# Multi-head attention on one core: the reciprocals' broadcast as four copies, the last set's lines on VectorE, and another order of the closing products

## The chip, the cores and the metric

The kernel runs on one core of one Trainium2 chip. The metric is the device time of one execution in microseconds. A core has TensorE (PE) for matrix products, VectorE (DVE), ScalarE (ACT) and GpSimd (POOL) for elementwise work, and SyncE (SP), which issues DMA copies. ScalarE and GpSimd can issue DMA copies too. All engines run at once and wait for one another by semaphores. Each executes its own instructions in the order in which the program has them.

## The reference

```python
B, S, D, H = 1, 2048, 448, 16          # bf16 inputs x, wqkv, wo
Dh = D // H                            # 28
qkv = (x @ wqkv).reshape(B, S, 3, H, Dh).transpose(2, 0, 3, 1, 4)
q, k, v = qkv[0], qkv[1], qkv[2]
scores = jnp.einsum("bhqd,bhkd->bhqk", q, k) * (Dh ** -0.5)
p = softmax(scores, axis=-1)
o = jnp.einsum("bhqk,bhkd->bhqd", p, v)
return o.transpose(0, 2, 1, 3).reshape(B, S, D) @ wo
```

## The kernel before

The sixteen heads form four groups of four (HG), each head in a band of 32 of the 128 partitions (HP). The 2048 queries form four chunks of 512 (QW). One group with one chunk of queries is a set; there are 16 sets (NSET), and the keys come in 16 tiles of 128. For each set, head and key tile TensorE makes a block of 128 x 512 scores (`emit_s`, L726), something turns it into weights of the softmax, and TensorE multiplies the weights by the values into one PSUM bank, the tile o (`do_pv`, L1069). One row of each head's band of o collects the sum of the weights, the softmax's denominator.

The weights are made in two ways. ScalarE takes two score blocks at once from the PSUM pairs a0 and a1 and writes exponentials into a tile pt (`do_exp`, L924); it does so 358 times, which is 716 of the 1024 blocks. VectorE makes the other 308 blocks from the banks d0, d1 and m: it writes the score as an integer that is the bit pattern of an approximate power (tile I, `do_a`, L939), and the weight is the sum of three such terms, each the first one with a number added to the integer. Four blocks of one set form a chain. The second and third term of a chain are the tiles called J. The third, and in some chains the second, is one addition on VectorE over four blocks (`do_add`, L1010). In the chains that are marked far, the second term is made elsewhere: GpSimd fills J with the number (`far_chain`, L975) and issues an accumulating DMA that adds I to it (`accumulate`, L986). A chain is far if at least FAR = 30 blocks of its set are left when it begins, and not in set 0.

When a set's products are complete, `finish_set` (L1084) queues its closing steps: VectorE copies o out of PSUM (`evac`, L1096); SyncE gathers the four denominator rows into a 128 x 16 tile (`gather`, L1101); VectorE takes reciprocals (`recip`, L1105); SyncE writes them to DRAM (`scatter`, L1110) and reads them back, each head's row repeated over its 32 partitions (`spread`, L1115, tile rr); GpSimd multiplies (`mul`, L1118) and writes the normalized output, tiles xs or OTL. Four of those, one for each group, are the input of the output projection of a query chunk (`oproj_job`, `quarters` at L301, bank m, VectorE's copy at L593, SyncE's store at L596).

The order of all instructions is written by a planner inside the kernel while the program is built. It keeps a clock for each engine, an estimated duration for each step and a time at which its result lands, and emits whatever can go next (`best`, `pick_pe`, `pick_dve` and so on, L1128 to L1244). `add` takes the step's cost, `land` the time until a DMA's result is there, `lag` a wait that is put before the step. A number changed in one step therefore moves the steps of all engines from there on. In `finish_set` the plan has these numbers: gather 0.6 and a landing of 3.0 (1.5 in the last two sets that are closed there), a lag of 2.5 before the reciprocal (0.3), scatter 0.35 and 1.1, spread 0.5 and a landing of 8.0 (6.0), multiply 1.3.

The last set (number 15) is not closed by `finish_set`. Near the end the planner queues early products of the output projection for the last query chunk, those of groups 0 to 2 (`early_jobs`, L1251), for four blocks of 128 queries in the banks d0, d1, m and one half of a pair. They start when fewer than 12 blocks are left for the first three, and when none is left for the fourth. The steps at L1285 to L1328 close the set: VectorE copies o in two halves, TensorE transposes the denominators (L1307), VectorE takes reciprocals (L1309), TensorE spreads them over the bands (L1313), VectorE multiplies (L1316, tile OTf), then whatever is left of the early products is emitted by `filler`, then TensorE adds group 3's product to each bank (L1323), VectorE and ScalarE copy the four banks out (L1325, L1327), and SyncE stores them in two pairs (L1328).

Of the kernel before, what the change touches and what calls it, by code (L numbers as in the profile page):

```python
# [39 lines left out]
def kernel(  # L40
# [7 lines left out]
    nc = tc.nc  # L48
# [4 lines left out]
    HP = 32  # L53
    G = 4
    HG = 4
    CC = 4
    CK = D // CC
    QW = 512
# [9 lines left out]
    XB = 4  # L68
# [9 lines left out]
    NJ = 4  # L78
    FAR = 30
    FIRST = 1  # L80
    AGE = 2.5
    SPLITQ = {1: ([0], [1, 2, 3]), 2: ([0, 1, 2, 3],), 3: ([0, 1, 2, 3],)}
    ACC_LAND = 5.6
    DRAIN = 10
    WARM = 0.52
    CL = NQC - 1
    NSET = G * NQC
# [7 lines left out]
    out_perm = out2.rearrange("(p t) d -> p t d", t=NKT)  # L95
# [140 lines left out]
    held = {}  # L236
# [3 lines left out]
    def add(eng, dur, emit, **k):  # L240
        op = Op(eng, dur, emit, **k)
        ops[eng].append(op)
        return op

    def ready(op):
        if cnt["step"] < op.gate or (op.acq == "m" and op.gives[0][0] == "O" and left() < 12):
            return None
        if op.acq == "m" and op.pri > 5 and ("KN0", NQC - 1) not in evt:
            return None
        r = 0.0  # L250
        for n in op.need:
# [513 lines left out]
    def left():  # L765
        return sum(len(q) for s in remain for q in remain[s])
# [39 lines left out]
    def d_more(s, t, acting):  # L806
        got, taken = [], []
        for b in d_banks(t):
            if not dve_ok(t, len(got)):
                break  # L810
            p = d_pick(s, t, acting, taken)
            if p is None:
                break
            step = take(*p)
            taken_by[step[0]][step[1]] += 1
            ch = chain["cur"]
            if ch is None:
                ch = chain["cur"] = {"I": wk.tile([P, HG * QW], I16, name="I4", bufs=NCH), "s": step[0], "n": 0,
                                     "got": [0] * NTERM, "m": None, "next": 0, "done": 0, "acc": 0.0, "far": False}
                chain["all"].append(ch)  # L820
                ch[1] = wk.tile([P, HG * QW], I16, name="J1", bufs=NJ)
                if sum(len(q) for q in remain[step[0]]) >= FAR and step[0] >= FIRST:
                    ch["far"] = True
                    far_chain(ch)
            taken.append(ch["next"])
            ch["next"] = 1 - ch["next"]
            ch["n"] += 1
            pd = bank_tile(b)
            got.append((b, pd, step, ch, ch["n"] - 1, max(t, res[b])))
# [254 lines left out]
    def finish_set(s, end):  # L1084
        g, c = set_gc(s)
        evt[("Oset", s)] = (end, "PE")
        cur["oset"] = s + 1
        cur["o_open"] = False
        o = cur["o"]
        if s == NSET - 1:  # L1090
            return
        st = {}

        def evac():
            st["o_sb"] = wk.tile([P, QW], F32, name="o_sb", bufs=2)
            nc.vector.tensor_copy(out=st["o_sb"][:], in_=o[:])  # L1096

        def gather():
            st["den"] = wk.tile([P, HG * QW // P], F32, name="den")
            n = P // HG  # L1100
            nc.sync.dma_start(out=st["den"][:], in_=st["o_sb"][Dh:P:HP, :].rearrange("i (p f) -> i p f", p=n))  # L1101

        def recip():
            st["rec"] = wk.tile([P, HG * QW // P], F32, name="rec")
            cur["shared"] = nc.vector.reciprocal(out=st["rec"][:], in_=st["den"][:])  # L1105

        def scatter():
            n = P // HG
            st["scr"] = dram.tile([HG, QW], F32, name="scr")
            nc.sync.dma_start(out=st["scr"][:].rearrange("h (p f) -> (h p) f", p=n), in_=st["rec"][:])  # L1110

        def spread():
            scr = st["scr"]
            st["rr"] = wk.tile([P, QW], F32, name="rr", bufs=1)
            nc.sync.dma_start(out=st["rr"][:], in_=scr[:].unsqueeze(1).to_broadcast([HG, HP, QW]))  # L1115

        def mul():
            m = nc.gpsimd.tensor_tensor(out=otile(g, c), in0=st["o_sb"][:], in1=st["rr"][:], op=ALU.mult)  # L1118
            after_shared(m)

        add("DVE", 0.61, evac, need=[("Oset", s)] + ([("OT",) + set_gc(s - 2)] if s > 1 else []), gives=[("osb", s)], rel="o", pri=-5)
        add("SP", 0.6, gather, need=[("osb", s)], gives=[("den", s)], land=3.0 if s < NSET - 2 else 1.5, pri=2)
        add("DVE", 0.16, recip, need=[("den", s)], gives=[("rec", s)], pri=50, lag=2.5 if s < NSET - 2 else 0.3, port=True)
        add("SP", 0.35, scatter, need=[("rec", s)], gives=[("scr", s)], land=1.1, pri=2)
        add("SP", 0.5, spread, need=[("scr", s)], gives=[("rr", s)], land=8.0 if s < NSET - 2 else 6.0, pri=2)
        add("POOL", 1.3, mul, need=[("rr", s)], gives=[("OT", g, c)], pri=60, port=True)

    def best(eng, t):  # L1128
# [119 lines left out]
    def late(op):  # L1248
        return op.gives and op.gives[0][0] == "O" and op.gives[0][1] == CL - 1

    def early_jobs(todo):  # L1251
        held.setdefault("early", [None] * XB)
        c = ORDER[-1][1]

        def mm(tq, bank, gg):
            if gg == 0:
                t = pair_tile(bank)[:, QW:2 * QW] if bank[0] == "a" else bank_tile(bank)[:]
                held["early"][tq] = t
            quarters(held["early"][tq][:, 0:D], otile(gg, c)[:, tq * P:(tq + 1) * P], WO[:, gg, :], gg == 0, False)

        for tq, bank in todo:
            for gg in range(G - 1):
                add("PE", 0.192, lambda tq=tq, bank=bank, gg=gg: mm(tq, bank, gg),
                    pri=2000 + tq, cols=D, need=[("OT", gg, c)] + ([("E", tq, gg - 1)] if gg else []), gives=[("E", tq, gg)],
                    acq=bank if gg == 0 else None)

    while cur["oset"] < NSET or ("E", 0) not in held or any(not late(op) and op.gives[0][0] != 'E' for e in ops for op in ops[e]) or any(k[0] == "O" for k in held):
        if left() < 12 and chain["cur"] is None and "early" not in held:
            early_jobs(enumerate(("d0", "d1", "m")))
        if left() == 0 and ("E", 0) not in held:  # L1270
            held[("E", 0)] = True
            early_jobs([(XB - 1, s_bank())])
        e = min(free, key=lambda n: free[n])
        t = free[e]
        end, nxt = pick[e](t)
        if end is not None:
            free[e] = end
            stuck = 0
            continue
        others = min(free[n] for n in free if n != e)  # L1280
        free[e] = max(t + 0.02, nmin(nxt, others))
        stuck += 1
        assert stuck < 40000, (t, cur, left(), pending, [(o.eng, o.need, o.acq) for q in ops.values() for o in q])
# [3 lines left out]
    o = cur["o"]  # L1287
    HW = QW // 2
    banks = held["early"]
    more = [op for op in ops["PE"] if op.gives[0][0] == "E"]  # L1290

    def filler(n):
        for op in more[:n]:
            op.emit()
        del more[:n]

    osb_last = [VT[1][0, hf].rearrange("p t e -> p (t e)").bitcast(F32) for hf in range(2)]
    rT = [wk.tile([P, 2, HG], F32, name=f"rT{hf}", bufs=1) for hf in range(2)]
# [11 lines left out]
    for hf in range(2):  # L1310
# [3 lines left out]
                                 lhsT=rT[hf][:, k, i:i + 1].to_broadcast([P, HP]), rhs=identf[:],  # L1314
                                 start=True, stop=True, tile_position=(0, HP * i))
        nc.vector.tensor_tensor(out=OTf[hf][:], in0=osb_last[hf], in1=work_ps[hf][:, HW:2 * HW], op=ALU.mult)  # L1316
    filler(12)
    rest = sorted({op.gives[0][2] for op in ops["PE"] if late(op)})
    for hf in range(2):
        osb = wk.tile([P, 2 * QW], BF16, name="pt", bufs=NPT)[:, 0:2 * D].rearrange("p (t d) -> p t d", t=2)  # L1320
        for k in range(2):
            tq = 2 * hf + k
            quarters(banks[tq][:, 0:D], OTf[hf][:, k * P:(k + 1) * P], WO[:, G - 1, :], False, True)  # L1323
            if k == 1:
                nc.vector.tensor_copy(out=osb[:, k, :], in_=banks[tq][:, 0:D])  # L1325
            else:
                nc.scalar.copy(out=osb[:, k, :], in_=banks[tq][:, 0:D])  # L1327
        nc.sync.dma_start(out=out_perm[:, c * XB + 2 * hf:c * XB + 2 * hf + 2, :], in_=osb)  # L1328
    for tq in rest:
        ps = pair_tile("a0" if tq % 2 else "a1")[:, 0:QW]  # L1330
        for gg in range(G):
# [38 lines left out]
```

## Time and profile before

| | us |
|---|---|
| three runs | 366.99, 363.5, 365.86 |
| median | 365.86 |
| the profiled execution | 365.38 |
| its span, first to last instruction | 363.5 |
| TensorE busy | 339.5 (93%) |
| VectorE busy | 333.4 (92%) |
| ScalarE busy | 340.8 (94%) |
| GpSimd busy | 174.8 (48%) |
| software DMA queue (GpSimd's) | 42.8% of 16 engines |
| SyncE's DMA queue | 9.9% of 16 engines |

The span leaves out 1.88 us of the profiled execution that lie around the first and the last instruction. Matmuls are pipelined, so TensorE's busy time says little by itself. In the views, a line has the start, the time it covers, the engine, the source line, the operation with its output and inputs, how many instructions are merged, and in brackets the idle time of the engine before it and what ended that. Idle time of an engine that is not the bottleneck costs nothing. Some of the steps that the change touches, as the profile has them:

| step | count | mean |
|---|---|---|
| L975 GpSimd fills J | 57 | 1064 ns |
| L986 GpSimd issues the accumulate of 512 KB | 57 | 915 ns; 4.9 us to landing (median) |
| L1010 VectorE adds, J from I | 97 | 758 ns |
| L1115 SyncE issues the broadcast of 256 KB | 15 | 554 ns (median) |
| L1118 GpSimd multiplies | 15 | 1415 ns for the 12 of tiles xs |

### The profile page before, as it was taken

What the parts mean: (1) busy time and instruction counts of PE and PEld (TensorE: products, weight loads), DVE (VectorE), ACT (ScalarE), POOL (GpSimd) and SP (SyncE); (2) the same over time, 40 slices, a digit from 0 to 9 for tenths busy, and PEclk for the clock granted to TensorE, in tenths of its full rate; (3) what the DMA queues carried; (4) which work ended last, traced back from release to release, by engine and by line L of the source; (5) the groups of instructions that cost most, each with busy time, mean ns of one, the idle gap of its engine ahead of it and who ended that gap; (6) DMA issues with size and microseconds to landing.
All of it is one profiled execution on the core that took longest, in us unless ns stands there. A gap on an engine that the chain in (4) does not pass through costs nothing.

```text
span 363.5 us, 11157 instructions
## 1 busy us (share of the span) xinstructions
PE 339.5 (93%) x4500; PEld 110.4 (30%) x4500; DVE 333.4 (92%) x615; ACT 340.8 (94%) x373; POOL 174.8 (48%) x217
## 2 busy tenths in 40 slices
PE   8999999999999999999889999988789899999975
PEld 4433233322234233232222222222222222222223
DVE  7789999999999999999999899999899999999933
ACT  4689999999999999999999999999899999999961
POOL 8951453644534374545655465447445244544310
PEclk9999999999999999999999999999999999999988
DMA  8510064664636356463668463486847467585741
GB/s 248 134 44 14 22 125 91 117 120 93 131 66 141 83 104 137 101 134 92 135 133 170 93 118 83 95 168 140 160 108 153 90 129 144 123 166 130 158 98 52
DMA packets 23260, 42.20 MB, mean 116 GB/s; under 512 B 7720, under 2 KB 13992, under 8 KB 23208
## 3 DMA queue, kind: packets, MB, share of 16 engines
q0 software_dynamic: 8720, 30.29, 42.8%
q1 hardware_dynamic: 13448, 10.18, 9.9%
q10 hardware_dynamic: 1040, 1.02, 0.9%
q8 instruction: 35, 0.57, 0.7%
q14 instruction: 17, 0.14, 0.1%
HBM read 7.58 MB, written 1.96 MB: 26 GB/s over the span
## 4 chain that ended last, share of the span: by engine, by line
ACT 39%; PE 30%; DVE 15%; issue 8%; DMA 6%; POOL 0%; DVEq 0%; ACTq 0%
ACT pt L924 38%; PE a L726 11%; PE o L1069 8%; DVE I L939 6%; DMA J<-I 5%; PE m L301 5%; DVE J L1010 3%; PE m L294 3%; DMA xs<-in_x_dram 1%; DVE KA L334 1%; DVE V L575 1%; DVE V L562 1%; DVE QA L456 1%; PE a L294 1%; PE d L301 1%
## 5 line engine op out<-in xcount | busy, mean ns | idle before, releaser
L924 ACT ACTIVATE pt<-a 128x1024 bf16<-128x1024 f32 x358 | 329.5, 1134 | 3.6 <-PE d L726 2.5
L939 DVE TENSOR_SCALAR I<-d 128x512 int16<-128x512 f32 x279 | 182.1, 681 | 9.9 <-PE d L726 8.5
L726 PE MATMUL a<-QP,KA 32*128 32x512 bf16 (+1 forms) x704 | 137.2, 381 | 12.3 <-ACT pt L924 11.4
L1069 PE MATMUL o<-pt,V 128*32 128x512 bf16 x716 | 105.4, 386 | 0.0
L726 PE MATMUL d<-QP,KA 32*128 32x512 bf16 (+1 forms) x274 | 96.8, 383 | 0.0
L726 PEld LDWEIGHTS <-KA 32*128 32x128 bf16 (+1 forms) x1041 | 46.0, 91 | 146.2 <-issue 144.8
L986 POOL DMA_DIRECT2D J<-I x57 | 52.1, 915 | 76.7 <-DVE I L939 55.2
L1069 PE MATMUL o<-J,V 128*32 128x512 bf16 x616 | 80.2, 386 | 4.0 <-DMA J<-I 4.0
L975 POOL MEMSET J<- 128x1024 int32 x57 | 60.3, 1064 | 48.7 <-DVE J L1010 17.8
L1010 DVE TENSOR_SCALAR J<-I 128x2048 int16<-128x2048 int16 x97 | 72.3, 758 | 0.2
L1069 PE MATMUL o<-I,V 128*32 128x512 bf16 x308 | 67.6, 384 | 0.7 <-DVE o_sb L1096 0.6
L1069 PEld LDWEIGHTS <-V 128*32 128x32 bf16 x1640 | 30.8, 95 | 52.3 <-issue 44.1
L316 POOL TENSOR_TENSOR sq<-QA 128x512 bf16<-128x512 bf16 x15 | 16.5, 1102 | 28.7 <-DVE QA L456 25.4
L294 PE MATMUL m<-XT,WRAW 112*32 112x512 bf16 x384 | 29.8, 384 | 0.2 <-DVE QA L456 0.2
L1118 POOL TENSOR_TENSOR xs<-o_sb,rr 128x512 bf16<-128x512 f32 x12 | 17.0, 1415 | 13.2 <-DMA rr<-scr 8.4
L301 PE MATMUL m<-WRAW,XT 112*32 112x112 bf16 (+1 forms) x768 | 20.7, 230 | 0.3 <-DVE KA L334 0.3
L939 DVE TENSOR_SCALAR I<-m 128x512 int16<-128x512 f32 x29 | 19.8, 681 | 0.2 <-PE m L726 0.2
L316 POOL TENSOR_TENSOR sq<-KA 128x512 bf16<-128x512 bf16 x12 | 14.8, 1235 | 4.7 <-DVE J L1010 3.8
L301 PEld LDWEIGHTS <-XT 112*32 112x32 bf16 x768 | 12.3, 96 | 11.5 <-issue 11.4
L301 PE MATMUL m<-WO,xs 128*32 128x448 bf16 x156 | 12.0, 359 | 0.0
L456 DVE CAST QA<-m 128x512 bf16<-128x512 f32 x15 | 10.3, 685 | 1.1 <-PE m L294 1.1
L726 PE MATMUL m<-QP,KA 32*128 32x512 bf16 (+1 forms) x29 | 11.2, 385 | 0.0
(116 smaller groups left out, 204.2 us busy)
## 6 DMA issues: line engine op xcount, KB each, us to landing
J<-I POOLq DMA_DIRECT2D x57, 512.0 KB, 4.9
rr<-scr SPq DMA_DIRECT2D x15, 256.0 KB
QP<-QA SPq DMA_DIRECT2D x60, 28.0 KB
out_dram<-osb SPq DMA_DIRECT2D x12, 112.0 KB
WRAW<-in_wqkv_dram SPq DMA_DIRECT2D x3, 392.0 KB
xs<-in_x_dram ACTq DMA_DIRECT2D x4, 224.0 KB
xs<-in_x_dram SPq DMA_DIRECT2D x4, 224.0 KB
QP<-su SPq DMA_DIRECT2D x32, 2.0 KB
```

Of the source, the lines that this page charges most:

```text
L294: nc.tensor.matmul(out=ps[HP * i:HP * (i + 1), :], lhsT=w[:, cc, h * Dh:h * Dh + HP], rhs=XT[c][cc // 2][:, cc % 2, :], start=(cc == 0), s ...
L301: nc.tensor.matmul(out=out[r, :], lhsT=lhsT[:, r], rhs=rhs, start=start, stop=stop, tile_position=(0, HP * i), **k)
L316: after_shared(nc.gpsimd.tensor_tensor(out=t[:], in0=src, in1=src, op=ALU.mult))
L456: nc.vector.tensor_copy(out=t[:], in_=held[key][:, 0:QW])
L726: nc.tensor.matmul(out=out_ap, lhsT=KAt[(g, j // XB)][r, (j % XB) * P:(j % XB + 1) * P], rhs=q[r, :], start=(n == 0), stop=(n == len(terms ...
L924: nc.scalar.activation(out=pt[:], in_=ps[:], func=ACT.Exp, scale=LN2 / 128.0)
L939: nc.vector.tensor_scalar(out=dst, in0=pd[:], scalar1=BIAS, scalar2=0.0, op0=ALU.add, op1=ALU.max)
L975: m = nc.gpsimd.memset(ch[1][:].bitcast(I32), fill)
L986: after_shared(nc.gpsimd.dma_start(out=ch[1][:, w], in_=ch["I"][:, w], accum_op=ALU.add))
L1010: cur["shared"] = nc.vector.tensor_scalar(out=r[:, w], in0=ch["I"][:, w], scalar1=float(SHIFT[k]), scalar2=None, op0=ALU.add)
L1069: nc.tensor.matmul(out=o[HP * i:HP * (i + 1), :], lhsT=VT[e["k"]][g, j // XB][:, j % XB, HP * i:HP * (i + 1)], rhs=e["ap"], start=(SETMM[k ...
L1118: m = nc.gpsimd.tensor_tensor(out=otile(g, c), in0=st["o_sb"][:], in1=st["rr"][:], op=ALU.mult)
```

## The change

The broadcast of the reciprocals is issued as four copies, one for each head, in place of one copy whose source has the outer sizes 4 and 32. Its numbers in the plan become a cost of 2.2 and a landing of 5.0 in all sets. The lag before the reciprocal becomes 4.0 (2.0 for the last two sets closed there), and the gather's landing is 3.0 everywhere. In the last set no chain is far: both J terms of all chains are VectorE's lines. Products of the output projection of earlier chunks may take bank m until fewer than 4 blocks are left (12 before), and the early products of bank m are queued only then. In the closing steps the early products that are left are emitted bank by bank: those of banks d0 and d1 before group 3's products, those of the third and the fourth bank each directly before its own. The two last blocks are stored one by one, the third from ScalarE's queue and the fourth from SyncE's.

```diff
+    RECLAG = 4.0
+    OLAST = 4
+    LASTFAR = 99
+    RR_LAND = 5.0
...
     def ready(op):
-        if cnt["step"] < op.gate or (op.acq == "m" and op.gives[0][0] == "O" and left() < 12):
+        if cnt["step"] < op.gate or (op.acq == "m" and op.gives[0][0] == "O" and left() < OLAST):
             return None
...
-                if sum(len(q) for q in remain[step[0]]) >= FAR and step[0] >= FIRST:
+                if sum(len(q) for q in remain[step[0]]) >= (FAR if step[0] < NSET - 1 else LASTFAR) and step[0] >= FIRST:
                     ch["far"] = True
                     far_chain(ch)
...
         def spread():
             scr = st["scr"]
             st["rr"] = wk.tile([P, QW], F32, name="rr", bufs=1)
-            nc.sync.dma_start(out=st["rr"][:], in_=scr[:].unsqueeze(1).to_broadcast([HG, HP, QW]))
+            for i in range(HG):
+                nc.sync.dma_start(out=st["rr"][HP * i:HP * (i + 1), :], in_=scr[i:i + 1, :].to_broadcast([HP, QW]))
...
-        add("SP", 0.6, gather, need=[("osb", s)], gives=[("den", s)], land=3.0 if s < NSET - 2 else 1.5, pri=2)
-        add("DVE", 0.16, recip, need=[("den", s)], gives=[("rec", s)], pri=50, lag=2.5 if s < NSET - 2 else 0.3, port=True)
+        add("SP", 0.6, gather, need=[("osb", s)], gives=[("den", s)], land=3.0, pri=2)
+        add("DVE", 0.16, recip, need=[("den", s)], gives=[("rec", s)], pri=50, lag=RECLAG if s < NSET - 2 else 2.0, port=True)
...
-        add("SP", 0.5, spread, need=[("scr", s)], gives=[("rr", s)], land=8.0 if s < NSET - 2 else 6.0, pri=2)
+        add("SP", 2.2, spread, need=[("scr", s)], gives=[("rr", s)], land=RR_LAND, pri=2)
...
-            early_jobs(enumerate(("d0", "d1", "m")))
+            early_jobs(enumerate(("d0", "d1")))
+        if "early" in held and ("E", "m") not in held and (left() < OLAST or not any(op.gives[0][0] == "O" for op in ops["PE"])):
+            held[("E", "m")] = True
+            early_jobs([(2, "m")])
...
-    more = [op for op in ops["PE"] if op.gives[0][0] == "E"]
-
-    def filler(n):
-        for op in more[:n]:
+    more = sorted((op for op in ops["PE"] if op.gives[0][0] == "E"), key=lambda op: op.gives[0][1:])
+
+    def filler(n, to=XB):
+        for op in [op for op in more if op.gives[0][1] < to][:n]:
             op.emit()
-        del more[:n]
+            more.remove(op)
...
-    filler(12)
     rest = sorted({op.gives[0][2] for op in ops["PE"] if late(op)})
     for hf in range(2):
...
             tq = 2 * hf + k
+            filler(XB * G, tq + 1 if hf else 2)
             quarters(banks[tq][:, 0:D], OTf[hf][:, k * P:(k + 1) * P], WO[:, G - 1, :], False, True)
...
-        nc.sync.dma_start(out=out_perm[:, c * XB + 2 * hf:c * XB + 2 * hf + 2, :], in_=osb)
+            if hf == 1:
+                (nc.sync if k else nc.scalar).dma_start(out=out_perm[:, c * XB + tq, :], in_=osb[:, k, :])
+        if hf == 0:
+            nc.sync.dma_start(out=out_perm[:, c * XB:c * XB + 2, :], in_=osb)
```

In the built program ScalarE's 358 exponentials and VectorE's 308 score blocks stay. The accumulates go from 57 to 55 and so do the fills of J, VectorE's J lines from 97 to 99, and TensorE has 20 more matmuls of zeros. The order differs on VectorE from the first set's reciprocal on.

More of the change, by code (lines that the diff above doesn't have):

```diff
@@ L1265, in early_jobs @@
                     acq=bank if gg == 0 else None)
-    while cur["oset"] < NSET or ("E", 0) not in held or any(not late(op) and op.gives[0][0] != 'E' for e in ops for op in ops[e]) or any(k[0] == "O" for k in held):
+    while cur["oset"] < NSET or ("E", 0) not in held or ("E", "m") not in held or any(not late(op) and op.gives[0][0] != 'E' for e in ops for op in ops[e]) or any(k[0] == "O" for k in held):
         if left() < 12 and chain["cur"] is None and "early" not in held:
-            early_jobs(enumerate(("d0", "d1", "m")))
+            early_jobs(enumerate(("d0", "d1")))
+        if "early" in held and ("E", "m") not in held and (left() < OLAST or not any(op.gives[0][0] == "O" for op in ops["PE"])):
+            held[("E", "m")] = True
+            early_jobs([(2, "m")])
         if left() == 0 and ("E", 0) not in held:
```

## The prediction

> **What bounds the kernel now.** I read the page first (busy times, groups), then ScalarE's timeline, the waits of TensorE, the chain of the last 20 us, the stretches with their granted clock, and the DMA queues in short stretches.
>
> ```profile
> PE 339.5 (93%) x4500; PEld 110.4 (30%) x4500; DVE 333.4 (92%) x615; ACT 340.8 (94%) x373; POOL 174.8 (48%) x217
> ...
> L924 ACT ACTIVATE pt<-a 128x1024 bf16<-128x1024 f32 x358 | 329.5, 1134 | 3.6 <-PE d L726 2.5
> ```
>
> Three engines are over 90% busy, so the shares alone decide nothing. ScalarE's timeline does:
>
> ```profile
> 131.52 88.11 ACT L924 ACTIVATE pt<-a 128x1024 bf16<-128x1024 f32 x96 [0.25 <-PE a L726]
> 219.88 41.54 ACT L924 ACTIVATE pt<-a 128x1024 bf16<-128x1024 f32 x45 [0.26 <-PE a L726]
> 263.00 88.55 ACT L924 ACTIVATE pt<-a 128x1024 bf16<-128x1024 f32 x96 [1.57 <-PE d L726]
> 359.18 0.53 ACT L1327 CAST pt<-d 128x448 bf16<-128x448 f32 x1 [7.63 <-PE d L301]
> ```
>
> From 18.86 to 351.55 ScalarE runs exponentials end to end, one every 0.92 us (88.55/96), with one real hole of 1.57 us before 263.00. So the span is a start of 18.86, a stream of 332.7, and a tail of 11.95 (351.55 to 363.5). Only holes in the stream and the tail can give time. TensorE's waits name the cause of both:
>
> ```profile
> 259.58 0.40 PE L1069 MATMUL o<-J,V 128*32 128x512 bf16 x4 [0.54 <-DMA J<-I]
> 262.18 0.39 PE L1069 MATMUL o<-J,V 128*32 128x512 bf16 x1 [1.34 <-DMA J<-I]
> ```
>
> ```profile
> 352.58 0.62 PE L1069 MATMUL o<-J,V 128*32 128x512 bf16 x4 [2.10 <-DMA J<-I]
> ```
>
> These are all of its waits for an accumulating copy (4.0 us on the page, three times). The same copy (J<-I) is the longest piece of the chain that ended last:
>
> ```profile
> 343.84 8.70 DMA J<-I
> 352.54 0.04 issue
> 352.58 1.04 PE o L1069 x8
> ```
>
> TensorE's clock is halved behind that wait: its matmuls take 0.62 to 0.64 us there against 0.39.
>
> ```profile
> 348.00:352.00 4.00, 2.49 (x30) 0.65 (x26) 0.55 (x1) 3.55 (x4) 1.26 (x1) 1.00 0.34 82
> 352.00:355.50 3.50, 2.92 (x32) 1.19 (x32) 0.64 (x2) 0.00 (x0) 0.00 (x0) 0.51 0.00 2
> ```
>
> (The last columns are clock, DMA share, GB/s.) Why do those copies land late? Issued from 253.5 to 254 and from 343.8 to 344, J<-I took 8.4 and 8.7 us to land; the median is 4.9. Both times a reciprocal broadcast (rr<-scr) was under way, issued at 250.73 and 340.78. A stretch in which a broadcast is nearly alone shows its width:
>
> ```profile
> q1 hardware_dynamic: 131, 0.26, 24.6%
> ```
>
> That is the SyncE queue from 143.57 to 146.32: the 256 KB in 2.75 us at a quarter of 16 engines' time. The broadcast uses 4 engines; each carries 32 of its 128 packets (24.6% x 16 x 2.75 / 131 = 83 ns each). An accumulate is spread wide and is done when its slowest engine is, so it waits for those four.
>
> **The change, part by part.** The profiled execution took 365.38 us for a span of 363.5 (1.88 around it), 0.48 under the median of 365.86; the sum goes against 365.38.
>
> *Broadcast as four copies.* The nearest row to a copy with many rows outermost is the final pair of stores (128 rows each); in the 40 slices of 360 to 363.5 the DMA share stands at eight and nine tenths while they pass, so they use all 16 engines:
>
> ```profile
> DMA  0000000000499998999999995000000000000000
> ```
>  Between the ends of 4 and 16 I take 16, since 32 rows on both sides resemble the store more than a source whose outer size is 4. Then an engine carries 8 packets, 0.7 us instead of 2.7, and an accumulate beside it is late by at most that. The holes at 259.58 and 262.18 go: -1.6 (ScalarE's 1.57). Ends: -2.8 (all of the small holes of 0.19 to 0.42 before other stretches go too) and +1.6 (the new order meets one collision more).
>
> The Trainium skill (DMA: Bandwidth & Descriptors, section on why a DMA increments its semaphore by 16) says that the engine count is the largest number up to 16 that divides the slowest dimension of both sides. By it the count is 4 now, which the 24.6% bears out, and 16 after, and the sum is the one above. Its rules for kernel authors speak the other way: coalesce, as transfers under 64 KB are mostly overhead. These are four of 64 KB, at the edge; by that rule rival E gains weight.
>
> What it costs: 45 more issues on SyncE at 0.55 us, 1.65 per broadcast. The densest stretch of that queue runs from 218.82 to 242.55, where the broadcast at 241.96 is last; the next issue is at 245.14, so 1.65 fits. Elsewhere the queue waits (58.2 us for o_sb, 54.6 for rec), and what stands behind a broadcast is a store, a gather or QP rows for a later set. I take 0; the upper end is 1.65 once, where QP rows stand behind it. GpSimd's multiply waits for the last copy. Issue to multiply took 7.1 (250.73 to 257.82), 8.5 and 8.9 us where it waited. With three quarters of a transfer of 2.75 to 4.2 us gone and 1.65 added, 6.7 to 7.4, against 7.2 (2.2 + 5.0) in the new plan and 8.5 in the old. So the plan fits, and accumulates queued behind the multiply on GpSimd's queue are not held.
>
> *New order.* RECLAG, land times and OLAST move nearly every instruction after set 0, but not the work: 358 exponentials and 308 VectorE score blocks stay, 20 zero matmuls are added (five groups of 0.23, into gaps). I take 0, with -1.0 to +1.6 as its ends (the small holes, and one large hole, as above).
>
> *Last set on VectorE.* Two memsets (1.06), two accumulates (0.92) leave GpSimd; two J lines of 0.76 come to VectorE: 1.5 us. VectorE's last J line ended at 348.55 and it then sat idle for 6.31, so its lines would end near 350.1, before the last exponential (351.55): 0 as long as that idle is there. Nothing waits for an accumulate in the tail any more. What is late next is the last exponential itself. In the new order TensorE has after its last score pair 14 products of the last set, 12 of the output projection, and then the last two exponentials' products, with 12 further projection products beside the copy of o. Before, o's copy began at 354.86, 3.31 after the last exponential. After, two products (0.39, started 0.17 late) and the copy's start: 0.6 as an estimate, ends 0.45 and 1.5. Gain: -2.7, the half clock (about 1.2 of it) included.
>
> *The end's products bank by bank.* Bank m's 12 products now run before the chain of reciprocals, so they leave it. OTf is ready at 358.25; in the old order TensorE went through 24 projection products until 358.89 and the last copy ended at 360.54 (5.68 after o's copy began). In the new one the two d banks start behind the first OTf half (3.1 after o's copy), m's product at 3.5, 12 products of bank a in 0.57, its last four by 4.6, and VectorE's copy ends at 5.3: -0.35, ends 0 and -0.5.
>
> *Stores.* The last store now carries 112 KB instead of 224 and the other went 0.9 earlier. The two now pass in 1.2 us together; the last alone needs 0.3 of that, but the issue and the landing stay: -0.3, ends 0 and -0.6.
>
> **Sum:** 365.38 - 1.6 - 2.7 - 0.35 - 0.3 = 360.4.
>
> **Rivals.**
> - B, the stream has a hole elsewhere: a new order can put an accumulate against other traffic. For it: small holes stand in every stretch. Against: the three waits for J all lie beside a broadcast. One hole of 1.6 to 3.2 instead: 362.0 to 363.6, say 362.8.
> - C, the clock falls in the tail without the wait: TensorE thins out behind the last scores anyway (2.49 of 4 us busy in 348 to 352). Half speed for 2.5 us costs 1.2: 361.6. The Trainium skill (TensorE: Matmul & The Clock Gate, section on why this matters) only warns of gaps over about 3 us; here the clock fell with a gap of 2.10, so the trace disagrees, and if the wait was not the cause, C holds.
> - D, VectorE's idle at the end is not there in the new order: its last J line ends after the last exponential, TensorE waits 1.5 and its clock halves (1.2): 363.1.
> - E, slower: the four copies don't overlap. Then the part of the trip that isn't transfer (7.1 - 2.75 = 4.35) is paid more than once, the multiply holds GpSimd's queue, the accumulates behind it go out late, and TensorE waits, as at 262.18. It decides from a trip of about 8.7 us (1.5 beyond the plan). One hole of 1.57 in 14 sets is 22: 382 with the tail's gains gone.
>
> **Numbers.** A 0.58 (360.4), B 0.18, C 0.09, D 0.08, E 0.07. About 1% is what a measurement can tell from no change here (the three runs spread from 363.5 to 366.99), so faster means under 362.2: nearly all of A, most of C, a third of B, a little of D: 0.68. Slower is E, 0.07; the rest, 0.25, is within 1%. The range leaves out E and the ends of A and B: 358.7 (A with the small holes gone) to 364.2 (B or D with 0.6 to 1.1 more).
>
> **What would show it.** Right: no broadcast stretch at a quarter share; J<-I landing under 6 us everywhere and no TensorE wait for it over 0.5; ScalarE without a hole over 1 us; o's last copy within 1 us of the last exponential and a granted clock of 1.00 there; the last copy 5.3 behind it. Wrong: GpSimd waiting for rr in many sets (E), TensorE waiting for VectorE's J at the end (D), a clock near 0.5 in the tail (C), or a stream from first to last exponential that is not shorter than 332 us (B).

## The result, and the profile after

| | before | after |
|---|---|---|
| median of six executions each | 366.36 us (363.5 to 367.99) | 361.91 us (361.72 to 362.93) |
| profiled execution | 365.38 us | 361.72 us |
| its span | 363.5 us | 359.9 us |

The ratio is 0.9891, with a 95% interval from 0.9851 to 0.9931. The change made the kernel 1.1% faster. The forecast was 360.4, in a range of 358.7 to 364.2. Medians and ranges here and below are of all executions; the ratios leave out two slow ones, e2's 374.31 and 376.43 us.

To see where the 3.6 us of span came from, I cut both spans at the same four events: the start of the first exponential, the end of the last, the start of VectorE's copy of o, and the end of the last copy out of PSUM.

| piece (us) | before | after | change | forecast |
|---|---|---|---|---|
| start, up to the first exponential | 18.86 | 19.39 | +0.53 | none |
| stream of exponentials | 332.69 | 331.88 | -0.81 | -1.6 |
| last exponential to o's copy | 3.31 | 0.48 | -2.83 | -2.7 |
| o's copy to the last copy out (closing) | 5.68 | 4.96 | -0.72 | -0.35 |
| last copy out to the span's end | 2.96 | 3.19 | +0.23 | -0.3 |

The page after, busy times and the main groups:

```profile
PE 343.1 (95%) x4520; PEld 111.3 (31%) x4521; DVE 335.4 (93%) x617; ACT 341.1 (95%) x373; POOL 170.2 (47%) x213
...
L928 ACT ACTIVATE pt<-a 128x1024 bf16<-128x1024 f32 x358 | 329.7, 1129 | 2.9 <-PE a L730 1.3
...
L1073 PE MATMUL o<-J,V 128*32 128x512 bf16 x616 | 82.7, 384 | 0.0
```

The busy times are about as they were. What went is idle time: TensorE's products with J waited 4.0 us before, and wait 0.0 now. ScalarE's timeline has the stream (start, time covered, idle before in brackets):

```profile
139.51 26.70 ACT L928 ACTIVATE pt<-a 128x1024 bf16<-128x1024 f32 x29 [0.38 <-PE a L730]
166.46 1.02 ACT L928 ACTIVATE pt<-a 128x1024 bf16<-128x1024 f32 x1 [0.24 <-PE a L730]
167.89 151.94 ACT L928 ACTIVATE pt<-a 128x1024 bf16<-128x1024 f32 x165 [0.40 <-PE o L1073]
319.99 31.28 ACT L928 ACTIVATE pt<-a 128x1024 bf16<-128x1024 f32 x34 [0.16 <-PE d L730]
354.88 0.53 ACT L1335 CAST pt<-d 128x448 bf16<-128x448 f32 x1 [3.61 <-PE d L305]
```

The hole of 1.57 is gone: 165 exponentials run without a break over the place where it was. New small holes stand at 139.51, 166.46 and 167.89. In the tail the idle time ahead of ScalarE's copy fell from 7.63 to 3.61. The two stretches of the tail (us, PE, PEld, DVE, ACT, POOL busy, clock, DMA share, GB/s):

```profile
348.00:352.00 4.00, 3.99 (x62) 1.64 (x60) 0.76 (x2) 3.26 (x4) 1.27 (x1) 1.00 0.02 6
352.00:355.50 3.50, 3.39 (x70) 2.32 (x68) 2.18 (x7) 0.62 (x2) 0.00 (x0) 1.00 0.00 0
```

TensorE is busy for 3.99 of 4 us where it had 2.49, and the clock stays at 1.00 where it fell to 0.51. The DMA queues in 242.57 to 243.46, where one broadcast passes:

```profile
q1 hardware_dynamic: 191, 0.26, 85.9%
```

The same 256 KB pass in 0.89 us at 86% of 16 engines, where they took 2.75 us at 25%.

### The profile page after: what moved, and what is told of

Its sections match the earlier page's. It is cut to its first block, busy times and chain, and to the rows that moved or that the text cites. A ratio compares the mean times of both kernels' runs of the same rounds, so it can differ in the third digit from the quotient of the medians.

```text
span 359.9 us, 11256 instructions
## 1 busy us (share of the span) xinstructions
PE 343.1 (95%) x4520; PEld 111.3 (31%) x4521; DVE 335.4 (93%) x617; ACT 341.1 (95%) x373; POOL 170.2 (47%) x213
## 4 chain that ended last, share of the span: by engine, by line
PE 37%; ACT 30%; DVE 23%; issue 9%; DMA 1%; DVEq 0%; ACTq 0%
ACT pt L928 30%; PE a L730 12%; DVE I L943 10%; PE o L1073 10%; PE m L305 5%; DVE J L1014 5%; PE m L298 4%; DVE V L579 2%; DVE V L566 2%; DVE KA L338 1%; PE o L643 1%; PE d L730 1%; DVE QA L460 1%; DVE o_sb L1100 1%; PE d L621 1%
## 5 line engine op out<-in xcount | busy, mean ns | idle before, releaser
L730 PE MATMUL d<-QP,KA 32*128 32x512 bf16 (+1 forms) x273 | 95.7, 383 | 0.8 <-DVE I L943 0.2
L990 POOL DMA_DIRECT2D J<-I x55 | 49.6, 902 | 73.0 <-DVE I L943 49.6
L1073 PE MATMUL o<-J,V 128*32 128x512 bf16 x616 | 82.7, 384 | 0.0
L1014 DVE TENSOR_SCALAR J<-I 128x2048 int16<-128x2048 int16 x99 | 73.9, 764 | 0.6
L1073 PE MATMUL o<-I,V 128*32 128x512 bf16 x308 | 64.3, 384 | 0.1
```

Of the source, the lines that this page charges most:

```text
L730: nc.tensor.matmul(out=out_ap, lhsT=KAt[(g, j // XB)][r, (j % XB) * P:(j % XB + 1) * P], rhs=q[r, :], start=(n == 0), stop=(n == len(terms ...
L990: after_shared(nc.gpsimd.dma_start(out=ch[1][:, w], in_=ch["I"][:, w], accum_op=ALU.add))
L1014: cur["shared"] = nc.vector.tensor_scalar(out=r[:, w], in0=ch["I"][:, w], scalar1=float(SHIFT[k]), scalar2=None, op0=ALU.add)
L1073: nc.tensor.matmul(out=o[HP * i:HP * (i + 1), :], lhsT=VT[e["k"]][g, j // XB][:, j % XB, HP * i:HP * (i + 1)], rhs=e["ap"], start=(SETMM[k ...
```

## The experiments

Two theories could explain the result. W: the narrow broadcast delays the accumulates that go out beside it, and so made both the hole in the stream and the late accumulate of the tail; widening it is all that matters. L: the broadcast fixed the stream, as the prediction had it, while the tail was fixed by having no accumulate in the last set. They part on kernels that have one of the two edits. The later runs ask what the bank order, the plan's numbers and the single stores do. All pieces are from the profiled execution of each kernel.

| kernel | first exp | stream | to o's copy | closing | to the end | profiled |
|---|---|---|---|---|---|---|
| before | 18.86 | 332.69 | 3.31 | 5.68 | 2.96 | 365.38 |
| after | 19.39 | 331.88 | 0.48 | 4.96 | 3.19 | 361.72 |
| e1: before, four copies | 19.53 | 330.61 | 0.48 | 5.32 | 3.15 | 360.91 |
| e2: after, one copy | 18.91 | 337.64 | 0.48 | 4.96 | 3.01 | 366.81 |
| e3: before, last set on VectorE | 19.33 | 336.24 | 0.48 | 4.49 | 2.96 | 365.30 |
| e4: after, last set far | 18.87 | 332.12 | 0.48 | 5.28 | 3.14 | 361.72 |
| e5: after, four narrow copies | 19.02 | 341.71 | 0.48 | 4.96 | 3.22 | 371.14 |
| e6: after, fill first | 18.90 | 332.39 | 0.48 | 4.76 | 3.67 | 361.94 |
| e7: after, stores in pairs | 18.93 | 331.82 | 0.48 | 4.96 | 3.50 | 361.56 |
| f2: e4 with the old plan numbers | 19.03 | 330.94 | 0.48 | 5.47 | 2.77 | 360.46 |
| f3: f2, eight products earlier | 19.33 | 330.75 | 0.48 | 5.17 | 2.77 | 360.36 |
| g2: f2 with the new lag | 18.87 | 331.53 | 0.86 | 5.28 | 3.07 | 361.41 |

**Four copies alone** (e1). The kernel before, with the order of every engine unchanged:

```diff
-            nc.sync.dma_start(out=st["rr"][:], in_=scr[:].unsqueeze(1).to_broadcast([HG, HP, QW]))
+            [nc.sync.dma_start(out=st["rr"][HP * i:HP * (i + 1), :], in_=scr[i:i + 1, :].to_broadcast([HP, QW])) for i in range(HG)]
```

> The kernel before in its own order on every engine; only the broadcast is issued as four copies, with the old numbers left in the plan. Theory W (width: the old broadcast loads 4 of 16 engines, and the accumulates beside it are late for that): no J<-I copy lands later than 6 us, the hole of 1.57 us in ScalarE's stream goes, and so does TensorE's wait of 2.10 us at the end with its half clock; o's last copy begins within 1.2 us of the last exponential instead of 3.31. That is 1.6 and 2.3 less: 361.5 us for an execution like the profiled 365.38, ratio 0.989, as much as the whole change. Rival O (order: the new order and the last set's move to VectorE brought the gain, the form of the copy nothing): the hole and the wait stay within 0.5 us, 365 us, ratio 0.998 to 1.0.

Measured: 360.76 (360.44 to 360.91), ratio 0.9855 [0.9819, 0.9892]. ScalarE's timeline:

```profile
220.52 129.62 ACT L924 ACTIVATE pt<-a 128x1024 bf16<-128x1024 f32 x141 [0.25 <-PE a L726]
354.59 0.53 ACT L1327 CAST pt<-d 128x448 bf16<-128x448 f32 x1 [4.45 <-PE d L301]
```

The last 141 exponentials are one piece. Before, they were 45 and 96 with 1.57 us between. In 342.2 to 342.5 the last set's accumulate goes out, and the stretch behind it shows the clock:

```profile
J<-I POOLq DMA_DIRECT2D x1, 512.0 KB, 5.6
```

```profile
348.00:352.00 4.00, 3.91 (x54) 2.06 (x46) 1.00 (x4) 2.14 (x3) 0.00 (x0) 1.00 0.01 2
```

The accumulate is there, it is as far as before, and it lands in 5.6 us instead of 8.7. TensorE doesn't wait for it and its clock stays at 1.00. A broadcast is still beside it: its four copies are issued from 340.31 to 342.53. The slowest accumulate of this execution took 6.4 us, a little over the 6 that W had as its bound, and no product waits for one. So the broadcast alone took 2.08 us out of the stream and all 2.83 out of the tail's wait. That is W. L's tail gain is not needed.

The wide broadcast also steadies the kernel. The 59 executions of the kernel before that ran beside the experiments took 363.28 to 368.9 us, and the longer ones had the lower mean clock of TensorE: 363.28 to 364.73 in the 15 at 0.998 or more, 365.71 to 368.9 in the 14 at 0.989 or less. All executions with a wide broadcast, e1's among them, stand at 0.997 or more, and those of one kernel lie within 1.2 us; those with a narrow one spread over 3 us or more, with clocks under 0.99 among them. Against the executions of before at 0.998 or more, four copies gain about 3 us (363.79 in the median against 360.76).

**The bundle with one copy** (e2). The kernel after, in its own order:

```diff
-            for i in range(HG):
-                nc.sync.dma_start(out=st["rr"][HP * i:HP * (i + 1), :], in_=scr[i:i + 1, :].to_broadcast([HP, QW]))
+            rr_in = scr[:].unsqueeze(1).to_broadcast([HG, HP, QW])
+            nc.sync.dma_start(out=st["rr"][:], in_=rr_in)
```

> The changed kernel in its own order on every engine; only the broadcast is one copy again. Theory W: in a quiet stretch a broadcast takes 2.7 us at a quarter of 16 engines' time, J<-I copies beside it land after 6 us or more, GpSimd waits for rr, and at least one hole of 0.5 to 1.6 us opens in ScalarE's stream; the tail, which has no accumulate, stays at 8.6 us behind the last exponential: 362.3 to 363.5 us, ratio 0.990 to 0.993 to the kernel before, against 0.989 for the changed kernel. Rival O: the order keeps the accumulates clear of the broadcasts by itself, nothing opens: 361.7 to 361.9, ratio 0.989.

Measured: 368.36 (365.67 to 376.43), ratio 1.0058 [1.0023, 1.0093]. Without the wide broadcast the rest of the change is a loss, and a larger one than I expected. Its waits (us in total, times, longest):

```profile
POOL xs L1123 <- DMA rr<-scr: 7.9, 2, 4.5
...
PE o L1073 <- DMA J<-I: 5.1, 5, 1.8
```

```profile
130.65 36.82 ACT L928 ACTIVATE pt<-a 128x1024 bf16<-128x1024 f32 x40 [1.47 <-PE a L730]
...
204.09 48.80 ACT L928 ACTIVATE pt<-a 128x1024 bf16<-128x1024 f32 x53 [0.94 <-PE d L730]
253.87 8.39 ACT L928 ACTIVATE pt<-a 128x1024 bf16<-128x1024 f32 x9 [0.98 <-PE m L730]
263.27 6.52 ACT L928 ACTIVATE pt<-a 128x1024 bf16<-128x1024 f32 x7 [1.01 <-PE d L730]
270.61 85.94 ACT L928 ACTIVATE pt<-a 128x1024 bf16<-128x1024 f32 x93 [0.82 <-PE d L730]
```

Both effects of a narrow broadcast are there. Accumulates beside it are late (8.4 us to landing for the one issued at 246.0), and GpSimd's multiply waits for rr; this plan reckons with 7.2 us from issue to landing where the old one had 8.5. The new numbers don't fit the old copy.

**Four copies, still narrow** (e5). Is it the number of copies, or the sizes of the source?

```diff
-                nc.sync.dma_start(out=st["rr"][HP * i:HP * (i + 1), :], in_=scr[i:i + 1, :].to_broadcast([HP, QW]))
+                nc.sync.dma_start(out=st["rr"][HP * i:HP * (i + 1), :], in_=scr[i:i + 1, :].unsqueeze(1).to_broadcast([HG, HP // HG, QW]))
```

> The changed kernel in its own order, four copies, but each copy's source has the outer sizes 4 and 8 in place of 32. Theory W with the rule that the outermost size sets the engine count: each copy uses 4 engines, a broadcast's transfer takes some 2.7 us again at about a quarter of 16 engines' time, and J<-I copies beside it land after 6 us or more: time as with one copy, 362.3 to 363.5. Rival N (four pieces, each 64 KB, are what helps, or the outer size doesn't matter): the transfer stays at about 0.9 to 2 us with all engines, J<-I under 6 us: 361.7 to 361.9, ratio 0.989.

Measured: 369.57 (366.51 to 371.14), ratio 1.0095 [1.0061, 1.0128]. The same rows in the same four copies, with the source written as 4 by 8 in place of 32. From 279.06 to 281.75 a broadcast passes:

```profile
q1 hardware_dynamic: 144, 0.26, 25.4%
```

A quarter of the engines again, the holes are back (a stream of 341.71), and GpSimd waits for rr four times, 19.0 us in all. So it is the outermost size that counts, not the splitting. The loss is far over the 362.3 to 363.5 that I expected. In the profiled execution some 4.0 us of it are of another kind, in the third set:

```profile
73.71 0.37 PE L730 MATMUL d<-QP,KA 32*128 32x512 bf16 x1 [1.72 <-DVE I L943]
```

```profile
74.00:81.00 7.00, 6.65 (x101) 2.31 (x100) 5.23 (x10) 3.63 (x4) 2.05 (x3) 0.51 0.46 89
```

TensorE waited for VectorE once, and its clock was at half for the next 7 us. ScalarE has holes of 2.72 and three times 0.44 there. An operation on VectorE took 1.85 us ahead of that, where the two of its line took 1.08 together in after; why isn't settled. Without these 4.0 us the stream is some 5.8 longer than after's, as e2's is with one narrow copy (5.76).

**The last set far again** (e4). The kernel after, with accumulates in its last set:

```diff
-    LASTFAR = 99
+    LASTFAR = FAR
```

> The changed kernel with the last set's chains far again as in the kernel before, so four accumulates and fills more and four J lines on VectorE less; the order differs only in the last set. Theory W: with the wide broadcast the last accumulate lands within 5.5 us, before the last exponential, so TensorE waits for it less than 0.5 us and keeps its clock: within 0.7 us of the changed kernel, 361.2 to 362.6, ratio 0.987 to 0.991. Rival L (the accumulate's own latency at the end is what cost the tail): TensorE waits 1 to 2 us for J at the end, the clock halves, and 2 to 2.7 us of the tail's gain is gone: 363.8 to 364.5, ratio 0.995 to 0.997.

Measured: 361.74 (361.66 to 361.96), ratio 0.9885 [0.9845, 0.9925], the same as after. It has 59 accumulates where after has 55. The one issued last, at 339.59:

```profile
J<-I POOLq DMA_DIRECT2D x1, 512.0 KB, 6.0
```

It lands 0.5 us later than expected, but nothing waits for it, and o's copy starts 0.48 behind the last exponential, as in after. With a wide broadcast, moving the last set to VectorE is worth nothing.

**The last set on VectorE alone** (e3). The kernel before, one copy, with only the condition changed:

```diff
-                if sum(len(q) for q in remain[step[0]]) >= FAR and step[0] >= FIRST:
+                if sum(len(q) for q in remain[step[0]]) >= (FAR if step[0] < NSET - 1 else 99) and step[0] >= FIRST:
```

> The kernel before with only the last set's chains kept from being far: one broadcast copy, the old numbers. The planner then gives one chain of four blocks to ScalarE (360 exponentials instead of 358) and drops four accumulates. Theory L (the tail's wait is the accumulate's): no wait for J at the end, the clock stays at 1.00, o's last copy begins within 1 us of the last exponential, 2.7 us less there; the two exponentials cost 1.8, and the hole of 1.57 in the middle stays: 364.5 us, ratio 0.996 to 0.999. Rival V (VectorE's lines at the end are late instead): TensorE waits for VectorE's J at the end, the gain there is under 1 us, and the time is 366 us or more, ratio over 1.000.

Measured: 364.96 (363.22 to 366.45), ratio 0.9988 [0.9957, 1.0019], no difference. ScalarE's timeline:

```profile
263.99 2.11 ACT L924 ACTIVATE pt<-a 128x1024 bf16<-128x1024 f32 x2 [1.95 <-PE d L726]
266.71 70.10 ACT L924 ACTIVATE pt<-a 128x1024 bf16<-128x1024 f32 x76 [0.61 <-PE a L726]
```

The hole of the stream stays, since the narrow broadcast does. The tail's wait is gone (0.48), so L's cure works too, and the closing is 1.19 shorter. Of that, 0.36 comes without the edit in e1; the other 0.83 goes with the early products, which now all run ahead of the chain of reciprocals. But the stream is 3.55 longer. The planner gave ScalarE 360 exponentials in place of 358, which is 1.8 us at 0.92 each, and the holes above are 1.0 more than the one before: here TensorE's clock fell behind the stream's wait for J (0.66 from 262 to 264 us, 0.50 from 264 to 266), where in the profiled execution of before it stayed at 1.00. What the tail gained went back into the stream.

**The old plan numbers** (f2). e4 with the plan's lines of gather, recip and spread as they were before, and the new closing and stores kept:

```diff
+        add("SP", 0.6, gather, need=[("osb", s)], gives=[("den", s)], land=3.0 if s < NSET - 2 else 1.5, pri=2)
+        add("DVE", 0.16, recip, need=[("den", s)], gives=[("rec", s)], pri=50, lag=2.5 if s < NSET - 2 else 0.3, port=True)
...
+        add("SP", 0.5, spread, need=[("scr", s)], gives=[("rr", s)], land=8.0 if s < NSET - 2 else 6.0, pri=2)
```

> The changed kernel with the plan's old numbers for gather, reciprocal and broadcast, and the last set's chains far again; four copies, the new order of the closing steps and the new stores stay. It differs from the run with the last set far in the plan's numbers alone, and from the kernel before with four copies in the closing steps alone. Theory P (the new numbers give an order with more small holes): ScalarE's stream takes 330.6 us from first to last exponential as in the kernel before with four copies, against 332.1 with the new numbers; bank m's early products are not out of the way here, so the tail keeps 8.9: 360.4 to 360.9 us, ratio 0.984 to 0.987. Rival Q (the 1.2 us between those two kernels are a difference of executions or of the closing steps, not of the plan's numbers): 361.5 to 361.9, ratio 0.988 to 0.990, a stream near 332.

Measured: 360.26 (360.1 to 360.48), ratio 0.9872 [0.9848, 0.9896]. The stream is 1.18 us shorter than e4's and 0.94 shorter than after's. ScalarE's timeline of f2 from 131 us on:

```profile
131.67 88.11 ACT L928 ACTIVATE pt<-a 128x1024 bf16<-128x1024 f32 x96 [0.24 <-PE a L730]
220.03 45.94 ACT L928 ACTIVATE pt<-a 128x1024 bf16<-128x1024 f32 x50 [0.25 <-PE a L730]
266.18 83.79 ACT L928 ACTIVATE pt<-a 128x1024 bf16<-128x1024 f32 x91 [0.22 <-PE m L730]
```

Its three holes sum to 0.71, the four of after in this stretch to 1.18. The other half of the difference to after is in gaps too short for the view: 0.921 us for an exponential in after's longest piece (151.94/165), 0.918 in f2's (88.11/96).

**The lag alone** (g2). f2 with the lag before the reciprocal as in after:

```diff
-        add("DVE", 0.16, recip, need=[("den", s)], gives=[("rec", s)], pri=50, lag=2.5 if s < NSET - 2 else 0.3, port=True)
+        add("DVE", 0.16, recip, need=[("den", s)], gives=[("rec", s)], pri=50, lag=RECLAG if s < NSET - 2 else 2.0, port=True)
```

> The version with the plan's old numbers, the last set's chains far and four copies, with only the lag before the reciprocal set to the new 4.0 (2.0 in the last two). Theory P1 (the lag's new order makes the small holes): ScalarE's stream takes 331.8 us or more (330.9 with the old lag) and the time is 361.3 to 362, ratio 0.989 to 0.991. Rival P2 (any new order has its own small holes, the lag is nothing special): a stream anywhere between 330.5 and 333, with holes at other places than 138 and 166 us.

Measured: 361.28 (360.84 to 361.41), ratio 0.9877 [0.9829, 0.9925]. The stream of 331.53 lies between f2's 330.94 and e4's 332.12, so it has about half of the loss and misses the bound of P1. Its holes stand at 120.81, 139.41, 159.12 and 167.71 (0.16 to 0.34 us), two of them away from 138 and 166, so P2, that any new order has holes of its own, isn't excluded. Another 0.38 of this kernel's loss is in the tail: TensorE waits that long for GpSimd's multiply, which itself waited 6.1 us for rr until 349.11, and o's copy starts 0.86 behind the last exponential. The other numbers weren't tried apart.

**After and e1 again, on one chip** (h1, h2). Is the difference between them one of the chips that they ran on?

> The changed kernel itself, on one chip and side by side with the kernel before with four copies alone. Theory W+P (the width brings the gain, the new plan numbers give part of it back): 361.6 to 362.2 us, 0.9 to 1.4 us slower than the four copies alone, a stream near 331.9. Rival Q (the 1.15 us between their medians is a difference of chips and occasions): both within 0.4 us of one another.

> The kernel before with four copies alone, side by side with the changed kernel. Theory W+P: 360.4 to 361.0 us and a stream near 330.6 again. Rival Q: within 0.4 us of the changed kernel.

Measured: after 361.55 (361.14 to 361.82), ratio 0.9892 [0.9848, 0.9935]; e1 360.72 (360.49 to 361.32), ratio 0.987 [0.9831, 0.991]. The ranges overlap a little here, from 361.14 to 361.32: one execution of each kernel lies there. The medians are 0.83 apart, under the 0.9 to 1.4 of W+P and well over Q's 0.4. The streams repeat, 331.81 and 330.63. In the profiled executions e1's kernel started its first exponential 0.64 later (19.51 against 18.87), which hides part of the difference in the stream.

**All left products first** (e6). The kernel after, with one line ahead of the closing products, which are then no longer bank by bank:

```diff
+    filler(XB * G)
     rest = sorted({op.gives[0][2] for op in ops["PE"] if late(op)})
```

> The changed kernel with all early products that are left (12, those of bank a) emitted before group 3's products, as in the kernel before; everything else is unchanged. Theory A: the first product of bank d comes 0.2 to 0.3 us later, since the 12 fill part of TensorE's wait for OTf, and the last copy out ends within 0.2 us of where it did (4.96 us behind the start of o's copy): 361.7 to 362.2 us, ratio 0.988 to 0.990. Rival B (the bank order is what shortened the closing steps from 5.68 to 4.96): the last copy ends 0.4 us or more later.

Measured: 361.97 (361.62 to 362.1), ratio 0.9918 [0.9896, 0.994]. VectorE's last two copies, first of after, then of e6:

```profile
355.08 0.62 DVE L1333 CAST pt<-d 128x448 bf16<-128x448 f32 x1 [0.30 <-PE d L305]
356.09 0.62 DVE L1333 CAST pt<-a 128x448 bf16<-128x448 f32 x1 [0.38 <-PE a L305]
```

```profile
355.37 0.62 DVE L1334 CAST pt<-d 128x448 bf16<-128x448 f32 x1 [0.57 <-PE d L305]
355.91 0.61 DVE L1334 CAST pt<-a 128x448 bf16<-128x448 f32 x1
```

With the old order the first copy is later and the last one earlier, 4.76 behind o's copy against 4.96. The bank order doesn't shorten the closing. The total shows nothing, since the end behind the last copy was 0.48 longer in this execution.

**Stores in pairs** (e7). The kernel after, with both pairs stored as before:

```diff
-            if hf == 1:
-                (nc.sync if k else nc.scalar).dma_start(out=out_perm[:, c * XB + tq, :], in_=osb[:, k, :])
-        if hf == 0:
-            nc.sync.dma_start(out=out_perm[:, c * XB:c * XB + 2, :], in_=osb)
+        nc.sync.dma_start(out=out_perm[:, c * XB + 2 * hf:c * XB + 2 * hf + 2, :], in_=osb)
```

> The changed kernel with the last two blocks stored as one pair by SyncE, as before. Theory A (the landing of the last store, not its size or queue, sets the end): the span ends 3.0 to 3.2 us behind the last copy out, as with single stores (3.19): 361.6 to 362.2 us, ratio 0.988 to 0.990. Rival S (single stores save what half the bytes take): the end comes 0.3 us later, 3.5 us behind the last copy.

Measured: 362.04 (361.56 to 362.48), ratio 0.9921 [0.9899, 0.9944]. The end comes 3.50 behind the last copy, 0.31 later than in after, which is rival S's number. It can't be told: that piece runs from 2.96 to 3.50 over the kernels with pairs and from 2.77 to 3.67 over those with single stores, and the median times of e7 and after are 0.13 apart.

**Eight products earlier** (f3). f2, with eight of bank m's early products ahead of the d banks' last ones:

```diff
+    filler(2, XB - 1)
     rest = sorted({op.gives[0][2] for op in ops["PE"] if late(op)})
```

> The version with the plan's old numbers, the last set's chains far and four copies, in which 8 of bank m's 12 early products are emitted before the d banks' last products instead of behind them; they fit in the 0.36 us in which TensorE waits for OTf. Theory A: bank a's last copy begins 0.3 to 0.4 us earlier (its wait of 0.89 us for TensorE shrinks), the last copy ends 5.1 us behind the start of o's copy instead of 5.47: 359.8 to 360.1 us, ratio 0.985 to 0.987. Rival B: the end of the last copy isn't what the time follows to a few tenths (landing of the stores varies by as much): 360.2 to 360.5.

Measured: 360.01 (359.9 to 360.36), ratio 0.9844 [0.9792, 0.9897], the lowest median of all. VectorE waits 0.51 for bank a's product where f2 waits 0.89, and the closing is 5.17 against 5.47:

```profile
355.10 0.62 DVE L1334 CAST pt<-a 128x448 bf16<-128x448 f32 x1 [0.51 <-PE a L305]
```

The totals of the two kernels overlap, so the 0.3 us is shown for the closing alone.

## Why the prediction was right, and where it wasn't

The direction, the 1% and the size of the tail's gain came out. The sum was 1.3 us too low (360.4 against 361.72 of the profiled execution), and it credited the largest term, the tail's, to the wrong edit. That this term still came out in size is luck: the edit that the prediction had for it is worth 0 beside the wide broadcast, which cures the same wait. In the stream the broadcast gained more than I had (2.08, not 1.6) and the new order lost what I had put at nothing (1.27), so two errors made up for one another in part.

- **Broadcast as four copies (-1.6).** The mechanism was right and the term too small. Its share of engines went from 24.6% to 85.9%, the slowest accumulate in after took 6.9 us to land (I had set 6 as the sign, before had 8.7), and no product waits for one. Alone it is worth 2.08 us of stream and 3.19 of tail (e1: 2.83 of wait and 0.36 of closing). Of the 2.08, the holes in ScalarE's timeline make 1.60 (2.97 against 1.37 in sum), as forecast; the rest lies in gaps too short to be shown. The prediction had found the same cause behind both waits, and then counted it for one only. The Trainium skill's rule (DMA: Bandwidth & Descriptors, section on why a DMA increments its semaphore by 16) fits all three forms measured: 4 outermost rows gave 24.6% and, in e5, 25.4%, and 32 gave 85.9%. The Trainium skill's advice to coalesce (same title, section on rules for kernel authors) isn't tested by after against e2, which differ in width too. At the same width, e5's four copies and e2's one cost the stream about the same, e5's loss in the third set aside.
- **New order (0).** This step failed. The new numbers of the plan cost 1.27 us of stream (331.88 against e1's 330.61; 1.18 between e4 and f2). I had given +1.6 as the upper end and no reason to be at 0. No single wait carries it: it is spread over small holes and over gaps too short to be shown, as f2's timeline beside after's has it. Whether the numbers themselves do it, or any other order would, isn't shown.
- **Last set on VectorE (-2.7).** The tail's numbers came out (0.48 behind the last exponential where I had 0.6, clock 1.00), but this edit is worth 0: e4 without it has the same 0.48 and the same time. I had also taken two accumulates off the last set. It loses four, and the new order gives earlier sets two.
- **Bank by bank (-0.35).** Of the measured -0.72, half isn't order: e1, with the old closing steps, is at 5.32 against 5.68, because the projection products ahead of the transposes of the denominators no longer run at half clock. The transposes take as long as before, but begin 0.48 behind the start of o's copy (351.10 against 350.62) where they began 0.83 behind it (355.69 against 354.86). The other -0.36 agrees with my term in size, and comes from where I put it in part: bank m's 12 products now run before the chain of reciprocals. The bank order that gives the step its name costs 0.15 to 0.2 (f2 5.47 against e1 5.32, both with 24 products behind the reciprocals; after 4.96 against e6 4.76, both with 12).
- **Stores (-0.3).** Not resolved. The piece behind the last copy differs by up to 0.9 between executions with the same stores.
- **Start.** The +0.53 isn't the change's. The ten matmuls of zeros at the start took 3.65 us in the profiled execution of before and 4.45 in that of after, and 4.02 in another execution of after, whose first exponential began at 18.87.
- **Rivals.** E did not happen: GpSimd waits 0.5 us for rr in all, and where it waits, the trip from the first issue to the multiply took 5.5 us (266.90 to 272.39), less than the 6.7 to 7.4 that I had worked out. My price for E was not what its words say: 382 is 360.4 and 22 with the tail's gains kept, and 365.38 and 22 without them are 387. C did not: the clock stays at 1.00 in the tail of every kernel whose last accumulate wasn't late. D did not. B is true in part, as the small holes of the new order. The stream is only 0.12 under the 332 us that I had set as its mark.

What stays open is what in the new plan makes the stream's loss beyond the half that comes with the lag, and whether single stores end sooner.

## What to carry to other kernels

Look at the outermost size of a DMA's source too: with 4 rows outermost it ran on a quarter of the engines here, and wide transfers beside it landed some 3 us late, in places that seemed unrelated. When a change is a bundle, run each edit alone in the otherwise unchanged order, because two edits that each cure the same wait (e1 and e3) are worth one cure together. A planner's numbers are part of the program: a kernel whose numbers are nearer to the measured trip (7.2 against 8.5, where 5.5 was measured) can be slower, and e1, one line from the kernel before, beats the whole change by 0.8 to 1.2 us.

## What the runs showed of the hardware

The length of a single gap doesn't decide whether TensorE's clock falls. In e3 it halved behind a wait of 1.29 us, as the products' 0.61 us in place of 0.39 show:

```profile
262.74 0.61 PE L1069 MATMUL o<-J,V 128*32 128x512 bf16 x1 [1.29 <-DMA J<-I]
```

At the same place in before it did not fall behind a wait of 1.34 us (262.18), and in e2 not behind a longer one:

```profile
129.61 0.40 PE L1073 MATMUL o<-J,V 128*32 128x512 bf16 x4 [1.82 <-DMA J<-I]
```

It also halved behind 2.10 us (before, at 352.58) and, in e5, behind 1.72 us with another 0.35 soon after. How busy TensorE was in the 4 us up to the restart sorts these cases: 1.91 us (before, 352.58), 1.94 (e5, up to 74.43) and 2.02 (e3) where the clock fell, 2.12 (before, 262.18) and 2.18 (e2) where it stayed. Five cases so close together don't make a rule. The bound of about 3 us for a gap that the Trainium skill warns of (TensorE: Matmul & The Clock Gate, section on why this matters) is too wide for this kernel, and no run gives a sharper one.
